# Attention and MoE kernel on one core: q and k turned as pairs of tokens in 32-bit words, statistics in three operations, the hand order rewritten

## The chip, the core and the metric

The kernel runs on one core of one Trainium2 chip. The core has five engines with their own instruction streams: TensorE (PE; its weight loads are listed as PEld), VectorE (DVE), ScalarE (ACT), GpSimd (POOL) and SyncE (SP, which here only issues transfers), and 16 DMA engines between them and HBM. [...] The metric is the device time of one execution in microseconds (us).

## The reference

Two parts follow each other. The first is attention with 4 batches, 8 heads, 768 tokens and 64 dimensions per head; a query sees the 8 first tokens and the 96 last ones, with a bias that falls with the distance:

```
scores = scale * q @ k.T                      # scale = 1/sqrt(64)
is_global = pos[None, :] < 8
is_local  = (rel >= 0) & (rel < 96)           # rel = query - key
dist  = where(is_global & ~is_local, 96, abs(rel))
scores = where(is_global | is_local, scores - slopes * dist, -1e9)
a = softmax(scores);  attn = a @ v
```

Its output is laid out as x, 3072 tokens of 512 values. The second is a feed-forward part with SoLU and layer norm, w_in of 512x1024 and w_out of 1024x512:

```
h = x @ w_in
solu = h * softmax(h)
ln = (solu - mean) / sqrt(var + 1e-6) * g_ln
out = ln @ w_out                              # 3072 x 512, float32
```

## The kernel before, in words

The 3072 tokens are 24 tiles of 128, six per batch. Heads are handled as four pairs p0 to p3 per batch, since two heads of 64 fill the 128 partitions.

Attention. q and k of a head pair come in as float32 with 128 tokens groups on the partitions: partition g holds six tokens in a row (load_heads, L469). In the code `j` is the place of a token in its group, `h` the head, `d` the dimension. A **cast** (steps cast_q and cast_k) makes float16 of them, 768 or 1536 values a partition, on POOL, VectorE or ScalarE. A **turn** (turn_q, turn_k, L712) makes six TensorE transposes of 128x128, one for each j, so that dimensions are on the partitions and tokens along the row. A **copy** (evac_q, evac_k) takes the turned 768 values of a partition out of PSUM into qT or kT, on VectorE or ScalarE, and puts tokens back in order with a stride. All copies and casts are recorded at the helper's lines: L271 for ScalarE, L273 for VectorE, L275 for POOL. There are 32 turns with 192 products. Scores follow (L839, L854), the exponential (L862), the bias as a factor (L871), the scores of the eight global keys (gscores), sums, the logarithm of the sums in a high and a low part (lhi L960, l16 L968), their exponential (rexp L1006), the products with v (L1031, L1041) and the scaled copy xT (L1066).

Feed-forward. gemm1 (L1104) multiplies a tile of xT with w_in, 8 products of 512 columns in two column halves; ef (L1114, ScalarE) takes the exponential and its sum s0, u (L1117, VectorE) the product with h and its sum s1, sq (L1124 on ScalarE or L1128 on VectorE) the sum of squares s2. u is turned by a DMA transpose (L1133) for tiles 5 to 21, and by TensorE (turn_u, L1143) with a copy out (evac_u, the tile named `late`) for the others. Every few tiles, **stats** (L1160 to L1167, four operations on VectorE on three columns) and rstd (L1171, L1172, ScalarE) make the scale of the layer norm; gemm2 (L1189) multiplies with gw_out (w_out scaled by g_ln and with its mean taken off), osb (L1199 or L1202) scales, and a store (L1206) is issued by SP or ScalarE.

w_in arrives in four transfers (L602), one for each half of its columns (fh 0, 1) and of its rows (jj 0 is rows 0 to 255, jj 2 rows 256 to 511), into the float32 tile `late`, and each half of a quarter is cast to w_in_sb. gemm1 of the first six tiles runs column half 0 first and then half 1, as two steps. w_out (L613) is scaled with g_ln by `centre` (L634), for which two float32 products (part_mean L626, mean L631) and a turn of g_ln (L575) are made.

Order. Every piece of this work is a step with a number. A table written by hand, ORDER, lists the step numbers; the steps are emitted in this order, and each engine runs its own part of it. SLOTS gives the buffer that each step takes, ENGS the engine of a step that has a choice, and WARM puts extra products on a constant tile (busy16, L1215) at places in the order. No step moves at run time; an engine that waits for a step holds everything behind it.

Of the kernel before, what the change touches and what calls it, by code (L numbers as in the profile page):

```python
# [17 lines left out]
P = 128  # L18
# [46 lines left out]
"""  # L65
SLOTS = """
# [78 lines left out]
def kernel(  # L145
# [113 lines left out]
    def one(s, n=0):  # L259
        return acc[:, at(s, "one", n), :]  # L260
# [993 lines left out]
```

## Time and profile before

| | us |
|---|---|
| median of three runs (161.46, 162.16, 163.80) | 162.16 |
| the profiled execution's own time | 162.93 |
| its span, from the first to the last instruction | 161.1 |
| TensorE busy | 150.1 |
| VectorE busy | 130.4 |
| ScalarE busy | 123.0 |
| GpSimd busy | 52.4 |

The span lies inside the execution's time, with 1.8 us around it; sums are made against 162.93, and the profiled execution is 0.77 above the median. The mean granted TensorE clock was 0.999. A busy share of TensorE counts a product from its start to its modelled end, so products in a row overlap in it. Of a row of the groups: busy time and mean of one, then idle time ahead of them on their engine and what ended it.

### The profile page before, as it was taken

How to read it: one execution, taken by the hardware profiler on the slowest of the kernel's cores; microseconds unless marked ns; L12 is line 12 of the kernel's file. 1: busy time of each engine (PE TensorE's matmuls, PEld its weight loads, DVE VectorE, ACT ScalarE, POOL GpSimd, SP SyncE). 2: the span in 40 equal slices, each digit the busy share in tenths (PEclk: the TensorE clock that was granted, in tenths of full speed). 3: DMA queues.
4: the chain of work that ended last, by engine and by line, in shares of the span. 5: the costliest groups of instructions: out<-in, count | busy, mean ns of one | idle time of the engine just before them, and what ended most of it. 6: DMA issues, size and time to landing. Idle time of an engine off the chain costs nothing.

```text
span 161.1 us, 4916 instructions
## 1 busy us (share of the span) xinstructions
PE 150.1 (93%) x1953; PEld 82.7 (51%) x1953; DVE 130.4 (81%) x271; ACT 123.0 (76%) x206; POOL 52.4 (33%) x120
## 2 busy tenths in 40 slices
PE   5689989999999999989999999999999999999991
PEld 1448546246565467457555434664444644444560
DVE  6384486999999999999699999783999778687830
ACT  3669997799989989887989959785974625856541
POOL 8764246257555377246165411300400000000000
PEclk9999999999999999999999999999999999999999
DMA  5999999989999999999669959711634803759453
GB/s 139 307 360 324 294 280 384 344 261 301 340 323 312 365 207 235 338 329 254 164 132 184 156 112 271 209 69 65 125 74 93 220 17 65 194 44 167 121 195 130
DMA packets 58390, 34.26 MB, mean 213 GB/s; under 512 B 44920, under 2 KB 53376, under 8 KB 58368
## 3 DMA queue, kind: packets, MB, share of 16 engines
q1 hardware_dynamic: 57360, 32.26, 75.4%
q10 hardware_dynamic: 1008, 1.70, 2.9%
q8 instruction: 15, 0.25, 0.6%
q14 instruction: 7, 0.06, 0.1%
HBM read 23.20 MB, written 6.29 MB: 183 GB/s over the span
## 4 chain that ended last, share of the span: by engine, by line
PE 50%; DVE 20%; DMA 13%; SPq 5%; issue 5%; ACT 3%; POOL 1%; DVEq 0%; ACTq 0%
PE acc L1189 24%; PE acc L1104 13%; DMA late<-in_moe_w_in_dram 9%; DMA x<-in_q_dram 5%; DVE eb L871 4%; DVE uu L1117 4%; DVE xT L1066 3%; PE acc L712 3%; PE acc L1041 3%; SPq L471 3%; DVE qT L273 2%; PE acc L854 2%; DVE v L273 1%; DVE sqv L1128 1%; ACT ef L1114 1%
## 5 line engine op out<-in xcount | busy, mean ns | idle before, releaser
L1189 PE MATMUL acc<-gw_out_sb,late 128*128 128x512 f16 (+1 forms) x200 | 45.0, 371 | 0.4 <-DVE qT L273 0.4
L1104 PE MATMUL acc<-w_in_sb,xT 128*128 128x512 f16 x192 | 44.4, 379 | 0.2
L1117 DVE SCALAR_TENSOR_TENSOR uu<-ef,acc 128x1024 f16<-128x1024 f16 x24 | 29.1, 1214 | 8.6 <-ACT ef L1114 8.5
L1114 ACT ACTIVATE ef<-acc 128x1024 f16<-128x1024 f32 x24 | 24.7, 1028 | 10.3 <-PE acc L1104 7.7
L862 ACT ACTIVATE eb<-acc 128x960 f16<-128x960 f32 (+1 forms) x32 | 29.0, 947 | 1.2 <-PE acc L854 0.9
L1104 PEld LDWEIGHTS <-xT 128*128 128x128 f16 x192 | 18.0, 98 | 22.1 <-DVE w_in_sb L273 0.9
L1189 PEld LDWEIGHTS <-late 128*128 128x128 f16 x200 | 18.6, 98 | 20.9 <-issue 1.6
L275 POOL CAST x<-x 128x768 f16<-128x768 f32 x20 | 18.1, 918 | 14.8 <-DMA x<-in_k_dram 6.1
L712 PE MATMUL acc<-ident,x 128*128 128x128 f16 x192 | 16.2, 238 | 2.7 <-POOL pick L342 1.5
L871 DVE TENSOR_TENSOR eb<-eb,fb 128x960 f16<-128x960 f16 x24 | 17.9, 761 | 0.6 <-ACT eb L862 0.5
L1124 ACT ACTIVATE sqa<-uu 128x1024 f16<-128x1024 f16 x14 | 14.8, 1059 | 3.5 <-DVE uu L1117 3.4
L712 PEld LDWEIGHTS <-x 128*128 128x128 f16 x192 | 13.2, 107 | 7.0 <-issue 2.1
L1066 DVE TENSOR_TENSOR xT<-acc,rr 128x384 f16<-128x384 f32 x32 | 16.0, 547 | 0.8 <-PE acc L1041 0.8
L1041 PE MATMUL acc<-eb,v 64*64 64x160 f16 (+4 forms) x448 | 15.2, 220 | 0.7 <-DVE tick L1051 0.5
L1006 ACT ACTIVATE rr<-acc 128x768 f32<-128x768 f32 x16 | 12.4, 812 | 4.1 <-DVE xT L1066 2.2
L1041 PEld LDWEIGHTS <-v 64*64 64x64 f16 x448 | 12.6, 106 | 4.2 <-issue 3.0
L275 POOL CAST v<-v 128x704 f16<-128x704 f32 (+3 forms) x14 | 9.1, 651 | 13.8 <-DMA v<-in_v_dram 13.8
L1199 ACT ACTIVATE osb<-acc,rstd 128x512 f32<-128x512 f32 (+1 forms) x13 | 8.4, 659 | 6.6 <-PE acc L1189 5.9
L273 DVE COPY qT<-acc 128x768 f16<-128x768 f16 x11 | 10.4, 949 | 3.7 <-PE acc L712 3.7
L1128 DVE SCALAR_TENSOR_TENSOR sqv<-uu 128x1024 f16<-128x1024 f16 x10 | 13.2, 1316 | 0.2
L854 PE MATMUL acc<-qT,kT 64*64 64x160 f16 (+2 forms) x384 | 13.1, 234 | 0.0
L1031 PE MATMUL acc<-eg,vgz 64*64 64x384 f16 x64 | 10.4, 324 | 0.0
(116 smaller groups left out, 201.3 us busy)
## 6 DMA issues: line engine op xcount, KB each, us to landing
x<-in_q_dram SPq DMA_DIRECT2D x16, 384.0 KB, 5.5
x<-in_k_dram SPq DMA_DIRECT2D x16, 384.0 KB, 6.1
out_dram<-osb SPq DMA_DIRECT2D x17, 256.0 KB, 2.5
v<-in_v_dram SPq DMA_DIRECT2D x12, 192.0 KB, 3.4
w_out<-in_moe_w_out_dram SPq DMA_DIRECT2D x4, 512.0 KB, 5.6
late<-in_moe_w_in_dram SPq DMA_DIRECT2D x4, 512.0 KB, 6.3
v<-in_v_dram SPq DMA_DIRECT2D x12, 160.0 KB, 3.8
out_dram<-osb ACTq DMA_DIRECT2D x6, 256.0 KB, 2.1
```

What stands on the lines that cost most here:

```text
L273: nc.vector.tensor_copy(out=out, in_=in_)
L275: nc.gpsimd.tensor_copy(out=out, in_=in_)
L712: nc.tensor.transpose(out=pt[:, ts(j, P)], in_=a[:, j, ts(pp, P)], identity=ident)
L854: nc.tensor.matmul(out=sc[o : o + 64, par, col : col + n], lhsT=kk[r, BLK * c : BLK * c + BLK], rhs=qq[r, g0 : g0 + n], start=fresh, stop= ...
L862: ex["fn"] = (lambda ex=ex, qk=qk, gw=gw: nc.scalar.activation(out=eb[at(qk, "eb")][:, :, 0:gw], in_=big(qk)[:, :, 0:gw], func=AF.Exp, sca ...
L871: nc.vector.tensor_tensor(out=e, in0=e, in1=bass.AP(tensor=f.tensor, offset=f.offset, ap=[f.ap[0], f.ap[1], [0, 3], f.ap[2]]), op=ALU.mult)
L1041: nc.tensor.matmul(out=o_[64 * h : 64 * h + 64, gl : gl + m], lhsT=vv[r, v_at(vi, h, c), pair, :], rhs=view(eb[at(e_own[b, gi, pair], "eb" ...
L1066: nc.vector.tensor_tensor(out=xT[at(xt_own[b], "xT")][:, p, q0:q1], in0=one(av, d)[:, 0:w], in1=rr[at(re, "rr")][:, d, 0:w], op=ALU.mult)
L1104: nc.tensor.matmul(out=ph()[:, ts(fh, 512)], lhsT=xT[at(xt_own[b], "xT")][:, j, ts(t % NA, P)], rhs=w_in_sb[:, j, ts(fh, 512)], start=(j = ...
L1114: ex["fn"] = lambda g1=g1, t=t, ph=ph: nc.scalar.activation(out=ef[at(g1, "ef")], in_=ph(), func=AF.Exp, accum_out=s0[:, t : t + 1])
L1117: u["fn"] = lambda u=u, g1=g1, t=t, ph=ph: nc.vector.scalar_tensor_tensor(out=uu[at(u, "uu")], in0=ef[at(g1, "ef")], scalar=USC, in1=ph(), ...
L1189: nc.tensor.matmul(out=one(g2)[:, 0:wd], lhsT=uT[at(el_o, "uT")][:, c, :], rhs=gw_out_sb[:, c, sl_], start=(c == 0), stop=(c == NFC - 1))
```

## The change

Four things change, and the tables with them.

- The cast writes two neighbouring tokens' float16 values (`t`) side by side, as (h, j, d, t): a 32-bit word holds a dimension of two tokens. It reads the float32 tile with a step of 64 words for t.
- The turn takes these words as float32 and makes three transposes of 128x128 against a float32 identity (ident32, a new constant on POOL) instead of six of float16; product j writes its words with a step of three, so that tokens come out in order.
- The copy out of PSUM is 768 contiguous float16 values, where it read with a step before.
- stats squares s0 and s1 in one operation (they lie side by side in s01 now) and adds in two more: three operations instead of four; the logarithm in rstd takes a scale of 1/1024.
- ORDER, SLOTS, ENGS and WARM are new. There are 11 warm products instead of 22. Of the turn copies 18 are on VectorE and 14 on ScalarE in both; sq goes from 10 on VectorE and 14 on ScalarE to 15 and 9; casts of q and k from 5, 7 and 20 (VectorE, ScalarE, POOL) to 9, 6 and 17.

```diff
@@ constants and tiles
+    ident32 = sb.tile([P, P], FP32, name="ident32")
-    s0 = sb.tile([P, NT], FP32, name="s0")
-    s1 = sb.tile([P, NT], FP32, name="s1")
+    s01 = sb.tile([P, 2, NT], FP32, name="s01")
+    s01q = sb.tile([P, 2, NT], FP32, name="s01q")
+    s0, s1 = s01[:, 0], s01[:, 1]
...
+    id32_st = step("POOL", 640, -90500, [], lambda: constants_ident(ident32, 1.0), name="c_ident32")
@@ cast
                          x16[at(cs, "x16_")][:, 0:m].rearrange(
-                             "p (j h d) -> p j h d", j=run, d=D),
+                             "p (h j d t) -> p h j d t", j=run // 2, d=D, t=2),
                          x32[at(iss, "x32_")][:, 0:m].rearrange(
-                             "p (h j d) -> p j h d", j=run, d=D))
+                             "p (h j t d) -> p h j d t", j=run // 2, d=D, t=2))
@@ turn
-                        pt = one(tps).bitcast(FP16)
-                        a = x16[at(cs, "x16_")][:, 0:m].rearrange("p (j x) -> p j x", j=run)
-                        for j in range(run):
-                            nc.tensor.transpose(out=pt[:, ts(j, P)], in_=a[:, j, ts(pp, P)],
-                                                identity=ident)
+                        pairs = run // 2
+                        pt = one(tps)[:, 0 : P * pairs].rearrange("p (g j) -> p j g", j=pairs)
+                        a = x16[at(cs, "x16_")][:, 0:m].bitcast(FP32).rearrange("p (j x) -> p j x", j=pairs)
+                        for j in range(pairs):
+                            nc.tensor.transpose(out=pt[:, j], in_=a[:, j, ts(pp, P)], identity=ident32)
@@ copy out
-                        copy(ev["at"], dst[at(ow[0], dn, ow[1])][:, lo:hi].rearrange("p (g j) -> p g j", j=run),
-                             one(tps).bitcast(FP16)[:, 0:n].rearrange("p (j g) -> p g j", j=run))
+                        copy(ev["at"], dst[at(ow[0], dn, ow[1])][:, lo:hi], one(tps).bitcast(FP16)[:, 0:n])
@@ stats and rstd
-                a, c = va[:, lo:hi], vb[:, lo:hi]
-                nc.vector.scalar_tensor_tensor(out=a, in0=s1[:, lo:hi],
-                                               scalar=-1.0 / D_FF / D_FF, in1=s1[:, lo:hi],
-                                               op0=ALU.mult, op1=ALU.mult)
-                nc.vector.scalar_tensor_tensor(out=a, in0=s2[:, lo:hi], scalar=1.0 / D_FF,
+                a, x = va[:, lo:hi], s01[:, :, lo:hi]
+                nc.vector.tensor_tensor(out=s01q[:, :, lo:hi], in0=x, in1=x, op=ALU.mult)
+                nc.vector.scalar_tensor_tensor(out=a, in0=s01q[:, 1, lo:hi], scalar=-1.0 / D_FF,
+                                               in1=s2[:, lo:hi], op0=ALU.mult, op1=ALU.add)
+                nc.vector.scalar_tensor_tensor(out=a, in0=s01q[:, 0, lo:hi], scalar=eps * D_FF,
                                                in1=a, op0=ALU.mult, op1=ALU.add)
-                nc.vector.scalar_tensor_tensor(out=c, in0=s0[:, lo:hi], scalar=eps,
-                                               in1=s0[:, lo:hi], op0=ALU.mult, op1=ALU.mult)
-                nc.vector.tensor_tensor(out=a, in0=a, in1=c, op=ALU.add)
...
-                nc.scalar.activation(out=vb[:, lo:hi], in_=va[:, lo:hi], func=AF.Ln)
+                nc.scalar.activation(out=vb[:, lo:hi], in_=va[:, lo:hi], func=AF.Ln, scale=1.0 / D_FF)
@@ WARM (position in the order : bank : products)
-28:0:5 36:4:0 49:4:1 73:0:2 92:0:4 107:6:2 128:6:5 168:4:1 197:4:1 297:4:1
+27:0:4 38:4:0 49:4:1 61:4:0 87:4:1 150:5:5
```

The new lines shift those behind them by one to four: copies and casts are at L273, L275 and L277 after, the turn at L716, gemm1 at L1106, gemm2 at L1188, the squares at L1126 and L1130, the loads of w_in at L605.

What the new tables do is seen at two places. The first is SP, around the loads of w_in (`late`, L602). The names: x is a piece of q or k, v, vt and vgn are pieces of v, g is g_ln. Before:

```order
L471 DMA x_2_104<-in_q_dram 128x2x384
L485 DMA v_0_113<-in_v_dram 128x3x64 x2
L613 DMA w_out_72<-in_moe_w_out_dram 128x2x512 x2
L602 DMA late<-in_moe_w_in_dram 128x2x512
L500 DMA vgn<-in_v_dram 64x1x64
L602 DMA late<-in_moe_w_in_dram 128x2x512 x2
L500 DMA vgn<-in_v_dram 64x1x64 x2
```

After, the same place:

```order
L575 DMA g_76<-in_moe_g_ln_dram 8x128
L605 DMA late<-in_moe_w_in_dram 128x2x512
L616 DMA w_out_73<-in_moe_w_out_dram 128x2x512
L605 DMA late<-in_moe_w_in_dram 128x2x512
L502 DMA vgn<-in_v_dram 64x1x64
L616 DMA w_out_73<-in_moe_w_out_dram 128x2x512
L605 DMA late<-in_moe_w_in_dram 128x2x512 x2
L487 DMA v_0_114<-in_v_dram 128x3x64
```

Before, one load of w_in stands further ahead (issued at 15.35 us in the trace), then one, then two together; after, one, one, and two together, with the last pieces of w_out between them. The four quarters change their order too, which the rows don't tell but the step numbers do: before (fh 1, jj 0), (fh 0, jj 2), (fh 0, jj 0), (fh 1, jj 2); after (fh 1, jj 0), (fh 1, jj 2), (fh 0, jj 2), (fh 0, jj 0). On all queues the transfers that are issued ahead of the last of them are the same in number and bytes: ten of q and k, eight of v, four of w_out, four of w_in.

The second place is VectorE in the middle of the run, where the factors of a group of scores (eb), copies (qT, kT), and u (uu) alternate. Before:

```order
L871 TENSOR_TENSOR eb_136<-eb_136,fb 128x960
L871 TENSOR_TENSOR eb_139<-eb_139,fb 128x960
L1117 SCALAR_TENSOR_TENSOR uu_157,s_94<-ef_153,acc 128x1024
L273 COPY kT_122<-acc 128x768
L273 COPY kT_120<-acc 128x768
L1117 SCALAR_TENSOR_TENSOR uu_154,s_94<-ef_152,acc 128x1024
L273 COPY qT_124<-acc 128x768
L1117 SCALAR_TENSOR_TENSOR uu_155,s_94<-ef_153,acc 128x1024
L273 COPY late<-acc 128x1024
```

After:

```order
L873 TENSOR_TENSOR eb_138<-eb_138,fb 128x960
L275 COPY kT_121<-acc 128x768
L275 CAST x_2_112<-x_2_105 128x2x3x128
L873 TENSOR_TENSOR eb_133<-eb_133,fb 128x960
L275 COPY qT_125<-acc 128x768
L275 COPY qT_124<-acc 128x768
L275 COPY qT_128<-acc 128x768
L1119 SCALAR_TENSOR_TENSOR uu_158,s_94<-ef_154,acc 128x1024
L1119 SCALAR_TENSOR_TENSOR uu_156,s_94<-ef_153,acc 128x1024
L275 COPY kT_120<-acc 128x768
L1130 SCALAR_TENSOR_TENSOR sqv,s_96<-uu_158 128x1024
```

More copies of qT and kT stand in a row, a cast of x and a square are put between them, and the products u come behind three copies. Counted from the first gemm1 to 108 us of before, VectorE has 13 of these copies after and 12 before, 7 squares and 4, 5 casts of x and 2, 3 copies of turned u and 2; 1 lhi and 2; of the casts of v of 704 columns 1 and 4, and one shorter. ScalarE has 9 copies and 10, 5 squares and 8, 4 casts of x and 3, 2 copies of turned u and 3; 3 casts of v of 704 columns and 1. POOL has 12 casts of x and 17. TensorE's steps in that part are the same in both.

More of the change, by code (lines that the diff above doesn't have):

```diff
@@ L684, in do_heads @@
                     take=("x32_",), name=nm)
-                cs = step(("POOL", "DVE", "ACT"), (10 + m, 35 + 0.59 * m, 120 + 0.785 * m), t0 - 1200, [dma],
+                cs = step(("POOL", "DVE", "ACT"), (85 + m, 35 + 0.59 * m, 290 + 0.785 * m), t0 - 1200, [dma],
                           None, lat=(100, 130, 155),
@@ L693, in cast @@
                          x16[at(cs, "x16_")][:, 0:m].rearrange(
-                             "p (j h d) -> p j h d", j=run, d=D),
+                             "p (j h d t) -> p h j d t", j=run // 2, d=D, t=2),
                          x32[at(iss, "x32_")][:, 0:m].rearrange(
-                             "p (h j d) -> p j h d", j=run, d=D))
+                             "p (h j t d) -> p h j d t", j=run // 2, d=D, t=2))
                 cs["fn"] = cast
@@ L700, in do_heads @@
                     p = p0 + pp
-                    tps = step("PE", 15 + run * 53.4, t0, [cs, id_st], None,
+                    tps = step("PE", 15 + run * 53.4, t0, [cs, id32_st], None,
                                take="one", mode="f", name="turn_" + nm, lat=180, ni=2 * run)
@@ L708, in pe @@
                     def pe(tps=tps, cs=cs, pp=pp):
[L709 to L713 removed]
+                        pairs = run // 2
[3 more added lines that the diff above has]
+                            nc.tensor.transpose(out=pt[:, j], in_=a[:, j, ts(pp, P)], identity=ident32)
                     tps["fn"] = pe
                     n = P * run
[L716 removed]
+                    ev = step(("DVE", "ACT"), (70 + 0.53 * n, 120 + 0.745 * n), t0 + 500, [tps], None, lat=(140, 165),
                               free=[(tps, "one")], name="evac_" + nm)
                     def evac(ev=ev, tps=tps, ow=ow, dst=dst, dn=dn, n=n):
[L720 to L721 removed]
+                        copy(ev["at"], dst[at(ow[0], dn, ow[1])][:, lo:hi], one(tps).bitcast(FP16)[:, 0:n])
                     ev["fn"] = evac
@@ L1158, in stats @@
             def stats(lo=lo, hi=hi):
-                a, c = va[:, lo:hi], vb[:, lo:hi]
-                nc.vector.scalar_tensor_tensor(out=a, in0=s1[:, lo:hi],
-                                               scalar=-1.0 / D_FF / D_FF, in1=s1[:, lo:hi],
-                                               op0=ALU.mult, op1=ALU.mult)
-                nc.vector.scalar_tensor_tensor(out=a, in0=s2[:, lo:hi], scalar=1.0 / D_FF,
+                a, x = va[:, lo:hi], s01[:, :, lo:hi]
[3 more added lines that the diff above has]
+                nc.vector.scalar_tensor_tensor(out=a, in0=s01q[:, 0, lo:hi], scalar=eps * D_FF,
                                                in1=a, op0=ALU.mult, op1=ALU.add)
-                nc.vector.scalar_tensor_tensor(out=c, in0=s0[:, lo:hi], scalar=eps,
-                                               in1=s0[:, lo:hi], op0=ALU.mult, op1=ALU.mult)
-                nc.vector.tensor_tensor(out=a, in0=a, in1=c, op=ALU.add)
-            st = step("DVE", 620, tt + 5700, [chain[x][1] for x in grp], stats, name="stats", lat=200)
+            st = step("DVE", 465, tt + 5700, [chain[x][1] for x in grp], stats, name="stats", lat=200)
             def rs(lo=lo, hi=hi):
-                nc.scalar.activation(out=vb[:, lo:hi], in_=va[:, lo:hi], func=AF.Ln)
+                nc.scalar.activation(out=vb[:, lo:hi], in_=va[:, lo:hi], func=AF.Ln, scale=1.0 / D_FF)
                 nc.scalar.activation(out=rstd[:, lo:hi], in_=vb[:, lo:hi], func=AF.Exp,
```

1 line of the change is left out of this document (removed), and 94 rows, old and new, of tables (ENGS, ORDER, SLOTS).

## The prediction

> **What bounds the kernel now.** I read the page first: the engine totals, the slices, the chain that ended last.
>
> ```profile
> span 161.1 us, 4916 instructions
> PE 150.1 (93%) x1953; PEld 82.7 (51%) x1953; DVE 130.4 (81%) x271; ACT 123.0 (76%) x206; POOL 52.4 (33%) x120
> DVE  6384486999999999999699999783999778687830
> ACT  3669997799989989887989959785974625856541
> PEclk9999999999999999999999999999999999999999
> PE 50%; DVE 20%; DMA 13%; SPq 5%; issue 5%; ACT 3%; POOL 1%; DVEq 0%; ACTq 0%
> PE acc L1189 24%; PE acc L1104 13%; DMA late<-in_moe_w_in_dram 9%; DMA x<-in_q_dram 5%; DVE eb L871 4%; DVE uu L1117 4%; DVE xT L1066 3%; PE acc L712 3%; PE acc L1041 3%; SPq L471 3%; DVE qT L273 2%; PE acc L854 2%; DVE v L273 1%; DVE sqv L1128 1%; ACT ef L1114 1%
> ```
>
> The reader is to see that no engine bounds the whole: TensorE is busy 93% but holds half of the chain, VectorE a fifth, and the transfers of w_in 9% in one place. The clock stays full. So I cut the run into stages: before the first gemm1, attention and gemms together, and the gemms that are left.
>
> ```profile
> 0.00:32.00 32.00, 26.61 (x405) 15.39 (x406) 21.13 (x59) 24.24 (x33) 17.04 (x69) 1.00 0.98 304
> 32.00:108.00 76.00, 74.14 (x1127) 42.93 (x1125) 71.83 (x134) 68.78 (x115) 33.59 (x50) 1.00 0.93 243
> 108.00:161.00 53.00, 49.38 (x425) 24.35 (x423) 37.47 (x80) 30.02 (x58) 1.82 (x1) 1.00 0.48 115
> by line: PE acc L1189 17.1%; DMA late<-in_moe_w_in_dram 12.4%; DVE eb L871 9.3%; issue 8.5%; DVE xT L1066 7.9%; PE acc L712 7.8%; DVE uu L1117 7.5%; PE acc L1104 6.3%; DVE qT L273 5.1%; DVE v L273 3.7%; DVE kT L273 3.3%; ACT eb L862 2.7%; P
> ```
>
> The columns after the length are PE, PEld, DVE, ACT, POOL busy, clock, DMA share, GB/s. The first stage is filled by transfers (0.98), the middle has three engines nearly full at once, the last belongs to TensorE. The fourth row is the chain from 32 to 96 us alone: there the work goes from engine to engine, and the two strided copies (qT and kT, L273) hold 8.4% of 64 us, 5.4 us.
>
> **The start: a term of its own.** The change doesn't alter how much is loaded ahead of the last quarter of w_in, but it alters which quarter comes last. The rows: SP's issues of w_in, three pieces of the chain, two stretches of TensorE, and one piece more of the chain.
>
> ```profile
> 15.35 1.17 SPq L602 DMA_DIRECT2D late<-in_moe_w_in_dram  x1
> 21.85 0.96 SPq L602 DMA_DIRECT2D late<-in_moe_w_in_dram  x1
> 23.52 1.06 SPq L602 DMA_DIRECT2D late<-in_moe_w_in_dram  x2
> 24.11 7.96 DMA late<-in_moe_w_in_dram
> 32.12 0.62 POOL w_in_sb L275
> 32.79 2.32 PE acc L1104 x10
> 31.23 3.88 PE L1104 MATMUL acc<-w_in_sb,xT 128*128 128x512 f16 x16
> 34.95 0.38 PE L1215 MATMUL acc<-busy 128*128 128x512 f16 x1
> 39.93 3.45 PE acc L1189 x16
> ```
>
> Before, the last quarter to be issued is columns 512 to 1023 of rows 256 to 511, which the first gemm1 needs only from the seventh of its 16 products on (tiles 2 and 0): TensorE starts at 31.23, and the next step at 34.95. After, the last is columns 0 to 511 of rows 0 to 255, which the very first product needs. With as many bytes ahead of it, it lands at 24.11 + 7.96 = 32.07, is cast by 32.74, and the products start at 32.79; 16 of them take 3.45 (the row at 39.93), so they end at 36.24: 36.24 − 34.95 = **+1.3 us**. TensorE has the same steps ahead of this point in both, so nothing else fills the wait. If the load comes 1 us sooner, the term is 0.3; I keep 0.3 to 1.6.
>
> **The products.** Of 32 turns (one is a head pair's 768 tokens of q or k), 10 are ahead of the first gemm1, under transfers; 22 are in the middle stage.
>
> ```profile
> 56.32 1.18 PE L712 MATMUL acc<-ident,x 128*128 128x128 f16 x18
> 30.00 1.12 PE L631 MATMUL acc<-part,onesq 128*128 128x512 f32 x2
> 29.99 0.30 PEld L631 LDWEIGHTS acc<-part,onesq 128*128 128x128 f32 x2 [0.23 <-ACT part L271]
> L631 PEld LDWEIGHTS acc<-part,onesq x2: 186/188/189, 30.0 to 30.1; 128*128 128x128 f32 x2
> L631 PE MATMUL acc<-part,onesq x2: 592/644/697, 30.0 to 30.5; 128*128 128x512 f32 x2
> ```
>
> A turn before: 18 products in 1.18 us, less the last one's tail (some 0.22), over 17 gaps: 56 ns each, six make 336. A 32-bit product of 128x128 isn't in the trace; the nearest are two of L631, 512 columns wide. Their loads start 0.30 − 0.19 = 0.11 us apart, the products 1.12 − 0.59 = 0.53; without the load, 0.42 for 512 columns, a quarter of which is 105. If load and stream overlap, a product takes some 107 ns, three make 320; ends of the range are 56 (as f16: 168 a turn) and 105 + 110 = 215 (nothing overlaps: 645). I take 107, since the second load of L631 starts while the first product streams. 22 × (320 − 336) = **−0.35 us**. The warm products that go from behind 32 us (two, 3.45 / 16 = 0.216 us each, the one at 34.95 among them) give **−0.4**.
>
> **Copies, casts and squares in the middle stage.** Columns at the end: busy, mean ns of one.
>
> ```profile
> L273 DVE COPY qT<-acc 128x768 f16<-128x768 f16 x7 | 6.6, 947 | 0.0
> L273 DVE COPY kT<-acc 128x768 f16<-128x768 f16 x5 | 4.6, 945 | 0.0
> L273 DVE COPY late<-acc 128x1024 f16<-128x1024 f16 x2 | 1.4, 686 | 0.2 <-PE acc L1143 0.2
> L273 DVE CAST x<-x 128x768 f16<-128x768 f32 x2 | 1.2, 621 | 0.0
> L273 DVE CAST v<-v 128x704 f16<-128x704 f32 x4 | 3.5, 876 | 0.0
> L1128 DVE SCALAR_TENSOR_TENSOR sqv<-uu 128x1024 f16<-128x1024 f16 x4 | 5.8, 1456 | 0.0
> L960 DVE TENSOR_SCALAR lhi<-lns,mlo 128x384 f16<-128x384 f32 x2 | 0.8, 410 | 0.0
> L1165 DVE SCALAR_TENSOR_TENSOR vb<-s 128x3 f32<-128x3 f32 x4 | 0.6, 153 | 0.0
> L271 ACT COPY kT<-acc 128x768 f16<-128x768 f16 x6 | 4.8, 805 | 0.0
> L271 ACT COPY late<-acc 128x1024 f16<-128x1024 f16 x3 | 3.1, 1029 | 0.0
> L271 ACT CAST x<-x 128x768 f16<-128x768 f32 x3 | 2.5, 838 | 0.0
> L271 ACT CAST v<-v 128x704 f16<-128x704 f32 x1 | 0.8, 799 | 0.0
> L1124 ACT ACTIVATE sqa<-uu 128x1024 f16<-128x1024 f16 x8 | 8.5, 1062 | 1.5 <-DVE uu L1117 1.3
> L1124 ACT ACTIVATION_READ_ACCUMULATOR sqa<-uu 128x1 f32 x8 | 1.6, 200 | 0.0
> ```
>
> A contiguous VectorE copy of 768 from PSUM isn't here; that of 1024 took 686, so it lies between 515 (in proportion) and 686, and no gain leaves 947. I take 550: a part of the 686 is fixed. ScalarE gains nothing: 805 for 768 strided is as much per element as 1029 for 1024 contiguous.
> VectorE in the middle, counted from the two orders: copies, 13 × 0.55 instead of 12 × 0.946, −4.2; three more squares, 3 × 1.53 with their readout, +4.6; three more casts of x, +1.9; casts of v, three of 704 fewer and one short one more, −2.2; one more copy of u, +0.7; one lhi less, −0.4; in four groups of statistics an operation less, −0.6. Together −0.3.
> ScalarE: three squares fewer, 3 × 1.26, −3.8; one turn copy less, −0.8; one copy of u less, −1.0; one cast of x more, +0.8; two casts of v more, +1.6. Together −3.2.
> POOL gives five of its casts of x away; it was idle over half of the stage, so this is hidden. What VectorE gains on copies is thus spent on squares, and the gain appears on ScalarE, where the chain holds little. TensorE's steps in this stage are the same in both, and it was unbusy for 76.00 − 74.14 = 1.86 us; its busy time holds waits too, so more can go. I take half of the 3.5 us of both engines, **−1.75**, near that 1.86; the ends are 0 and −5.2 (all of ScalarE's 3.2 and 42% of the copies' 5.4, or 2.0; the saving of a copy is 0.4 of 0.95).
> The casts now read with a stride of 64 words and write word pairs. No cast of before does; I take the old durations, since ScalarE reads PSUM at a stride with no loss, and keep +0.4 us on each (what VectorE's strided copy loses, 947 against 550) as the other end: hidden on POOL, +2.0 on VectorE's five, some of it again on ScalarE's four, which has given 3.2 away. I see no reason for a gain, since the bytes read and written stay the same.
>
> **The last stage.** Statistics are three operations instead of four, 0.15 us by L1165, ahead of rstd and the outputs; the last tile's chain keeps its operations. TensorE's products set this stage, and I count nothing, within 1 us either way. One store more is issued by ScalarE instead of SP; ScalarE is busy 30.02 of 53.00 us here, which hides it. The new constant is built on POOL in the first stage, where it is busy 17.04 of 32.00; without that cover the first turns would start later by its length, and the transfers, not the turns, end that stage. The nine other warm products that go lie under the first stage's transfers.
>
> **Sum.** The profiled execution took 162.93 us, its span and 1.8 around it, 0.77 above the median of 162.16. 162.93 + 1.3 − 0.35 − 0.4 − 1.75 = 161.7; less 0.77, **160.9 us**. Two per cent, 158.9 and 165.4, is about what a measurement of this kernel can tell from no change.
>
> **The rivals.**
> *Forecast*, 159 to 163.5: chance 0.52, of which I put 0.01 below 158.9 and 0.03 above 165.4.
> *The copies were the chain.* If what leaves VectorE and ScalarE comes off the end whole, −5.2 stands for −1.75: 157.5. For it: VectorE is 71.83 of 76 busy, and qT and kT have no idle time ahead of them (0.0), they queue behind other work. Against it: the squares that VectorE takes over fill the same queue. 0.24.
> *A 32-bit product is slow.* At 215 ns each, 66 products in a stage where TensorE has 1.86 us free cost 66 × 0.108 = +7.1: 168.0, slower. It decides from some 68 ns above my 107, about 175 a product (4.5 / 66). For it: no product of before writes at a step of 12 bytes. Against it: the loads of L631 overlap. 0.14.
> [...]
> *Strided casts are slow.* +2.0 on VectorE: 162.9. 0.06.
> [...] The trace has no such cast; its strided copies out of PSUM lose time on VectorE and none on ScalarE.
> *The copy isn't faster.* If the price of 947 is that of 768 halfwords out of PSUM in that place, and no stride: 13 × 0.4 = +5.2, 166.1. 0.04.
>
> **Numbers.** Below 158.9 lie the second case and the forecast's lower edge: 0.24 + 0.01 = 0.25. Above 165.4 the third, the fifth and the upper edge: 0.14 + 0.04 + 0.03 = 0.21. Within, 0.48 + 0.06 = 0.54. The likeliest is 160.9; the range of 157.2 to 166.2 leaves out most of the slow product and the far end of the fast copies, some 0.2.
>
> **What would show it.** The products of L716 should start 107 ns apart; copies of L275 on VectorE take 515 to 686; casts of x about 620, 840 and 930 on the three engines; the first gemm1 starts near 32.8 behind the last quarter of w_in; and ScalarE's busy time in the middle falls by 3 us. I am wrong if L716 goes above 175, if the first gemm1 isn't held, or if chains in the middle close up beyond what ScalarE gave.

## The result, and the profile after

The changed kernel takes 168.7 us (median of five runs, 167.46 to 170.86) where before takes 162.31 beside it: a ratio of **1.034** (1.027 to 1.041), slower. The ratio compares the faster runs alone, three of these five and four of five of before, so it is a little below that of the medians. The profiled execution took 167.54 us against 162.93, its span 165.8 against 161.1. The forecast of 160.9 and its range up to 166.2 were both missed.

Lines of the changed kernel's page: the engines, the 40 slices of TensorE and of the transfers, the queue of instructions that is read below (packets, MB, share of the DMA time), and the chain of work that ended last:

```profile
span 165.8 us, 4718 instructions
PE 147.5 (89%) x1846; PEld 81.0 (49%) x1846; DVE 130.5 (79%) x275; ACT 118.9 (72%) x195; POOL 57.2 (35%) x121
PE   4669778699999799998699999889999999999991
DMA  5999989999899989999927999981395703846743
q8 instruction: 14, 0.23, 0.6%
PE 57%; DMA 20%; DVE 10%; issue 4%; ACT 3%; SPq 2%; POOL 0%; POOLq 0%; DVEq 0%; ACTq 0%
```

No engine became the bound: TensorE, VectorE and ScalarE all have a smaller share than before. VectorE's part of the chain halved (20% to 10%), that of the transfers grew (13% to 20%), and "issue", time in which the profile shows nothing to wait for, stands at 4% (5% before). The same stages as before show where TensorE lost its time:

```profile
0.00:32.00 32.00, 23.01 (x352) 12.74 (x352) 17.34 (x55) 20.18 (x27) 19.67 (x74) 1.00 0.94 295
32.00:108.00 76.00, 70.94 (x954) 40.53 (x950) 70.57 (x135) 65.65 (x108) 34.56 (x45) 1.00 0.99 234
108.00:166.00 58.00, 53.54 (x544) 27.75 (x544) 42.56 (x87) 33.04 (x61) 3.01 (x3) 0.99 0.54 122
```

In the middle TensorE is busy 70.94 us of 76 where it was 74.14, while the transfers go from 0.93 to 0.99 of their time. The stages are cut at the same times, so the change, which lags, has done less of its program in them: 954 products against 1127, of which the halved turns explain 66. That ScalarE's busy time falls by 3.1 us (65.65 for 68.78), as forecast, is therefore no measure of the saving.

The products and the copies came out as priced, the casts didn't. Rows of the groups on VectorE, ScalarE and GpSimd (32 to 108 us; the GpSimd row over 0 to 108), and one piece of the chain:

```profile
L275 DVE COPY qT<-acc 128x768 f16<-128x768 f16 x9 | 4.8, 548 | 0.3 <-PE acc L716 0.3
L275 DVE CAST x<-x 128x768 f16<-128x768 f32 x5 | 4.4, 884 | 0.0
L273 ACT CAST x<-x 128x768 f16<-128x768 f32 x5 | 5.0, 1004 | 0.0
L277 POOL CAST x<-x 128x768 f16<-128x768 f32 x17 | 18.0, 1067 | 10.5 <-PE acc L1106 3.8
84.75 0.98 PE acc L716 x9
```

A copy takes 548 ns instead of 947, a 32-bit product 0.98 / 9 = 109 ns, and the casts are slower than the 621, 838 and 918 ns of before (VectorE, ScalarE, GpSimd).

**Two waits have no cause in the profile.** What TensorE waited for (total, times, longest), and its timeline at the first of them:

```profile
PE acc L856 <- issue: 3.0, 2, 2.0
PE acc L716 <- POOL x L277: 2.7, 3, 1.7
PE acc L629 <- ACT rr L1008: 1.7, 1, 1.7
PE acc L1188 <- DMA late<-uu: 1.6, 2, 1.4
...
52.95 0.81 PE L856 MATMUL acc<-qT,kT 64*64 64x160 f16 x16
54.77 0.43 PE L856 MATMUL acc<-qT,kT 64*64 64x160 f16 x13 [1.01 <-issue]
```

In the middle of a run of score products TensorE stops, with nothing that would release it. Before has no such row. The records of the trace show what falls there. The queue `q8 instruction` carries packets of 16 KB, one for about 260 of TensorE's records (its products and weight loads, counted from 0: 3717 records, 14 packets; 3915 and 15 before), and both waits end behind the end of one of them. Start of the last product ahead and of the next record, the number of that record, and the packet:

```
kernel          wait              record   packet start + length   from its end to the next record
change          53.52 -> 54.77    1217     52.21 + 1.13            1.43 us
change          78.04 -> 80.23    1985     77.74 + 1.07            1.42 us
```

The two records are 768 apart, three times 256. This gives a theory to test, and no more than that: TensorE's own instructions come late here, since packets of them stand behind data. No row shows what these packets carry or that an engine waits for one.

### The profile page after: what moved, and what is told of

Read it like the earlier page. It is cut to its first block, busy times and chain, and to the rows that moved or that the text cites. A ratio compares the mean times of both kernels' runs of the same rounds, so it can differ in the third digit from the quotient of the medians.

```text
span 165.8 us, 4718 instructions
## 1 busy us (share of the span) xinstructions
PE 147.5 (89%) x1846; PEld 81.0 (49%) x1846; DVE 130.5 (79%) x275; ACT 118.9 (72%) x195; POOL 57.2 (35%) x121
## 4 chain that ended last, share of the span: by engine, by line
PE 57%; DMA 20%; DVE 10%; issue 4%; ACT 3%; SPq 2%; POOL 0%; POOLq 0%; DVEq 0%; ACTq 0%
PE acc L1188 20%; PE acc L1106 19%; DMA x<-in_k_dram 9%; DMA late<-uu 6%; DMA late<-in_moe_w_in_dram 5%; PE acc L1043 4%; DVE uu L1119 4%; PE acc L716 3%; PE acc L856 3%; DVE gw_out_sb L637 2%; ACT ef L1116 1%; PE acc L999 1%; PE acc L629 1%; DVE sqv L1130 1%; PE acc L939 1%
## 5 line engine op out<-in xcount | busy, mean ns | idle before, releaser
L1188 PE MATMUL acc<-gw_out_sb,late 128*128 128x512 f16 (+1 forms) x200 | 43.8, 371 | 2.1 <-DMA late<-uu 1.6
L1106 PE MATMUL acc<-w_in_sb,xT 128*128 128x512 f16 x192 | 44.8, 379 | 0.3 <-DVE uu L1119 0.2
L864 ACT ACTIVATE eb<-acc 128x896 f16<-128x896 f32 (+1 forms) x32 | 29.3, 957 | 4.7 <-PE acc L856 4.7
L1188 PEld LDWEIGHTS <-late 128*128 128x128 f16 x200 | 19.1, 98 | 23.1 <-DMA late<-uu 2.0
L1106 PEld LDWEIGHTS <-xT 128*128 128x128 f16 x192 | 18.1, 98 | 20.8 <-issue 1.1
L277 POOL CAST x<-x 128x768 f16<-128x768 f32 x17 | 18.0, 1067 | 10.5 <-PE acc L1106 3.8
L716 PE MATMUL acc<-ident,x 128*128 128x128 f32 x96 | 16.5, 299 | 3.5 <-POOL x L277 2.7
L1130 DVE SCALAR_TENSOR_TENSOR sqv<-uu 128x1024 f16<-128x1024 f16 x15 | 19.0, 1269 | 0.2
L277 POOL CAST v<-v 128x704 f16<-128x704 f32 (+3 forms) x12 | 9.5, 799 | 20.5 <-DMA v<-in_v_dram 15.4
L716 PEld LDWEIGHTS acc<-ident,x 128*128 128x128 f32 x96 | 11.3, 150 | 7.7 <-POOL x L277 3.9
L1043 PE MATMUL acc<-eb,v 64*64 64x160 f16 (+4 forms) x448 | 14.7, 219 | 0.3 <-ACT eb L864 0.3
L856 PEld LDWEIGHTS <-kT 64*64 64x64 f16 x384 | 8.8, 111 | 6.2 <-issue 5.0
L1201 DVE TENSOR_SCALAR osb<-acc,rstd 128x512 f32<-128x512 f32 x12 | 8.9, 748 | 3.0 <-PE acc L1188 2.4
```

The source lines that it names most:

```text
L277: nc.gpsimd.tensor_copy(out=out, in_=in_)
L716: nc.tensor.transpose(out=pt[:, j], in_=a[:, j, ts(pp, P)], identity=ident32)
L856: nc.tensor.matmul(out=sc[o : o + 64, par, col : col + n], lhsT=kk[r, BLK * c : BLK * c + BLK], rhs=qq[r, g0 : g0 + n], start=fresh, stop= ...
L864: ex["fn"] = (lambda ex=ex, qk=qk, gw=gw: nc.scalar.activation(out=eb[at(qk, "eb")][:, :, 0:gw], in_=big(qk)[:, :, 0:gw], func=AF.Exp, sca ...
L1043: nc.tensor.matmul(out=o_[64 * h : 64 * h + 64, gl : gl + m], lhsT=vv[r, v_at(vi, h, c), pair, :], rhs=view(eb[at(e_own[b, gi, pair], "eb" ...
L1106: nc.tensor.matmul(out=ph()[:, ts(fh, 512)], lhsT=xT[at(xt_own[b], "xT")][:, j, ts(t % NA, P)], rhs=w_in_sb[:, j, ts(fh, 512)], start=(j = ...
```

## The experiments

Each ratio is to runs of before taken beside it on the same chip; the change stands at 1.034.

### Which half of the change costs: the code or the tables

The step numbers of both kernels differ by the one new step (the identity), so each code runs under the other's ORDER, SLOTS, ENGS and WARM.

```diff
 e1_old_tables: changed cast, turn, copy, statistics
-ORDER, SLOTS, ENGS, WARM of the change
+ORDER, SLOTS, ENGS, WARM of before (c_ident32 set behind c_ident)
 e2_old_code: cast, turn, copy, statistics of before
-ORDER, SLOTS, ENGS, WARM of before
+ORDER, SLOTS, ENGS, WARM of the change (without c_ident32)
```

> The changed cast, turn, copy and statistics run under the tables of before (order, buffers, engines, warm products; the new identity stands behind the old one on POOL). If the word layout itself is what costs (strided casts, 0.26 us more on VectorE, 0.17 on ScalarE, 0.13 on POOL each), this is slower than before, 164 to 167 us. If the new tables are what costs, it is as fast as before or faster: 160.5 to 162.5 us, since copies save 0.4 us on VectorE 18 times. The first gemm1 should start near 31.2 us as before, and TensorE should have no wait of over 1 us for which the profile shows no releaser.

> The cast, turn, copy and statistics of before run under the tables of the change (without the step of the new identity). If the tables cost, this is slower than before by all of it or more: 166 to 170 us, with the first gemm1 near 34 us. If the word layout costs, it is near 162 us.

Measured: the new code under the old tables 1.003 (0.999 to 1.007), the old code under the new tables 1.042 (1.037 to 1.048). **The tables hold all of the loss.** The code by itself does not move the time under the old order; under the new one it reads 0.8% faster, with intervals that overlap. The middle stage of the new code under the old tables, and its copies:

```profile
32.00:108.00 76.00, 74.31 (x1063) 42.97 (x1062) 69.00 (x132) 68.85 (x115) 35.83 (x50) 1.00 0.94 243
L274 DVE COPY qT<-acc 128x768 f16<-128x768 f16 x7 | 3.8, 550 | 0.2 <-PE acc L715 0.2
L274 DVE COPY kT<-acc 128x768 f16<-128x768 f16 x5 | 2.7, 548 | 0.5 <-PE acc L715 0.5
```

VectorE does 2.8 us less (71.83 to 69.00), its copies now wait for TensorE, and TensorE is as busy as before: the gain is off the path.

How far a kernel lags behind before can be followed through the run, if the work of TensorE that has been done is summed from the starts of its products (columns by their pace, warm products left out) and the times at which two profiles have the same sum are subtracted (good to some 0.3 us):

```
us behind before, when before is at    32     44     72    104    end
change                                 2.6    2.0    2.6   5.6    4.6
e1_old_tables                          0.3   -0.2   -0.4  -0.3   -0.2
e2_old_code                            3.6    4.1    5.6   8.4    7.0
e4_shift176 (below)                    3.2    2.4    2.8   4.6    3.5
e6s_start_shift (below)                1.1    1.3    2.1   3.9    2.9
```

Some 2.5 us are lost by the first gemm1, about as much again in the middle.

### Are TensorE's instructions late?

If so, the wait belongs to a count of instructions and not to a product. Tiny products on TensorE ahead of the waits, in its first 10 us, of which it is busy 4.94 in the change, shift the count and change nothing else: 88 of them are 176 records, a product and its weight load each. The expectations call the counts at which the theory has the next packet due places of fetches; they are an estimate from the two records above, and no row shows such a place.

```diff
+            for _ in range(count // 1000):
+                nc.tensor.matmul(out=acc[0:32, spot, 0:8], lhsT=busy16[:, 0:32],
+                                 rhs=busy16[:, 0:8], start=True, stop=True)
```

> The changed kernel with 88 tiny products (32 columns loaded, 8 streamed) added on TensorE in the first 10 us, nothing else. [...] If the two waits without a releaser (1.2 us at 53.4 and 2.1 us at 78.0) are TensorE waiting for its instructions behind other transfers, both go, and the time falls by 2 to 3.3 us, less up to 1.5 for the products: 166 to 167.5 us. If they wait for data, they stay where they are and the time is 168.5 or above.

> The changed kernel with 48 tiny products instead of 88. By the places of the fetches, the first wait (53.4 us) goes and the second stays but comes earlier in the program, some 2 us ahead of its old place, at the 1889th instead of the 1985th of TensorE's old records, 1.5 to 3 us long. If they wait for data, both stay at the same products as in the change.

With 88 of them: 1.023 (1.018 to 1.029), 166.14 us, and none of its products has a wait of 0.2 us or more without a releaser. **A kernel with 176 more instructions is about 1% faster**: its four runs, 165.80 to 167.19 us, all lie below the five of the change. With 48: 1.033 (1.025 to 1.041), and one such wait, at the count that was expected:

```profile
PE acc L856 <- issue: 2.3, 1, 2.3
```

```
kernel          wait              record   packet start + length   from its end to the next record
e5_shift96      77.05 -> 79.55    1985     76.81 + 1.14            1.60 us
```

The record has the same number, 1985, and so stands 96 records earlier in the program than in the change; no data that it could need is the same. Wherever TensorE had such a wait of over 0.5 us in the middle of a row of products, the record behind it is number 193 + 256 n: 705 under the old code in the new tables (1.9 us from one start to the next), 961 in e7 below, 1217 and 1985 in e3, in e6 and in the kernel with the start of before. Kernels under the old tables have one too, at 1985 (e1 0.6 us, e8 1.0 us), and at ratios of 1.003 and 1.005 lose no time that can be told.

One of the two waits is gone here and the time is not lower. The trace shows something that the change's own profile doesn't have: behind the wait that is left TensorE's granted clock is at half for 3.4 us. That stretch, and the first eight products of gemm1 in it, with eight of the change behind its wait:

```profile
80.90:84.30 3.40, 3.40 (x32) 1.57 (x32) 3.40 (x4) 2.93 (x4) 3.40 (x4) 0.50 0.70 158
81.80 3.12 PE L1106 MATMUL acc<-w_in_sb,xT 128*128 128x512 f16 x8
82.85 1.90 PE L1106 MATMUL acc<-w_in_sb,xT 128*128 128x512 f16 x8
```

The profiles of e3 and e6 below have the same, with the clock at half for 3.4 us from 78.8 and from 81.8 us. Of the change's five runs four had a mean clock of 0.980 to 0.987, and in its profile it is 0.997; of the four with the 88 products none was below 0.996. Five of the runs of before beside these experiments had 0.979 and took 162.24 to 163.78 us, nothing lost that can be told, so the mean alone is no cost; but the eight products took 3.12 us at half the clock and 1.90 at the full one. The 1% may thus hold both, the stops and the clock behind them; the runs don't part the two.

The opposite test is to put such a wait into before.

```diff
 e7_before_shift: the kernel before
+96 tiny products in TensorE's first 9 us
```

> The kernel before, with 96 tiny products in TensorE's first 9 us and nothing else. [...] If late instructions cost time, TensorE gets waits without a releaser that before doesn't have, and the time rises by 1.5 to 4 us: 163.7 to 166.5 us. If they don't, it is within 0.6 us of before.

Measured 1.004 (0.999 to 1.008): not the 1.5 to 4 us expected, a term that no run shows. A stop of 1.9 us did come, at record 961 and 29.0 us, and the time doesn't show it; near 50 us a packet started at 49.13, and no product behind it has a wait of over 0.4 us without a releaser. In these runs the number of the record behind a stop could be told ahead, and whether a stop comes could not; what decides that is not shown.

### The start

> The changed kernel, with the quarters of w_in loaded in the order of before (the quarter that the first product needs is no longer last) and the first two casts of w_in behind the exponentials that TensorE waits for on ScalarE. If the start of the first gemm1 (33.9 us against 31.2) is carried to the end, this gains 1.5 to 2.7 us against the change: 165.5 to 167 us. If the later waits take it up, it stays within 0.7 us of the change.

In it the five warm products (27.5 us) came to write a PSUM bank that a spread of the attention part was using, so part of the output is spoilt; the work is the same. It ran at 1.029 (1.022 to 1.036), no clear gain, and the first gemm1 started at 33.71 instead of 34.03: the quarter and the two casts weren't alone in holding it. The next one mends three holds at once, with the warm products back in place.

```diff
-149 (fh1 jj0)  153 (fh1 jj2)  145 (fh0 jj2)  141 (fh0 jj0)
+149 (fh1 jj0)  145 (fh0 jj2)  141 (fh0 jj0)  153 (fh1 jj2)
-ScalarE: cast w_in, rexp, rexp, cast w_in, copy_mean, rexp
+ScalarE: rexp, rexp, cast w_in, copy_mean, rexp, cast w_in
-TensorE: gemm1 t2, gemm1b t2, gemm1 t0, gemm1b t0
+TensorE: gemm1 t2, gemm1 t0, gemm1b t2, gemm1b t0
```

> The changed kernel with a mended start: the quarters of w_in in the order of before, ScalarE's casts of them behind the exponentials that TensorE waits for, and the first gemm1 running column half 0 of tiles 2 and 0 ahead of half 1. If the start is held by these three, the first gemm1 starts at 32.3 to 33 us (33.9 in the change) and the time falls by 1 to 1.8 us, to 166 to 167 us in the runs of the change (a ratio to before of 1.023 to 1.028). If the attention ahead of it holds it, 33.5 us and nothing gained.

> The mended start and the 88 tiny products. If start and late instructions are two separate losses, both gains add: 2.5 to 3.5 us below the change, a ratio to before of 1.012 to 1.018. If one hides the other, it stays at the 1.023 of the kernel with the products alone.

Alone: 1.030 (1.021 to 1.039), not told from the change; in the traced execution (170.88 us) the first gemm1 starts at 33.59, later than expected. With the tiny products: 1.017 (1.011 to 1.024), the first gemm1 at 32.51. The two gains add in the ratios; against the 1.023 of the products alone the intervals overlap, so the start's share of 0.6% is only indicated.

Grafting the start of before onto the rest of the change, and the other way round, was to split the loss at the first gemm1. The rest keeps each engine's order; only steps that the other start had done already are left out, and buffers are given anew where they clash.

> The changed kernel, whose order, engines and buffers up to the first gemm1 are those of before; from there on each engine runs its steps in the order of the change. If the start loses 2.6 us that stay lost, this gains 2 to 3 us against the change: 165 to 166.5 us, with the first gemm1 near 31.2 us. If the middle would lose them anyway, it stays within 0.7 us of the change. The instruction stream of TensorE ahead of the cut is 18 records longer, so the two waits without a releaser (50 to 80 us) should still be there, 2.5 to 4.5 us together.

> The kernel with the start of before, and 79 tiny products more in the first 9 us of TensorE. If the two waits are late instructions, they go and this gains 2 to 3.5 us more: 162 to 164 us, as fast as before within 1 us. If they are not, it is as the kernel without the products or up to 1 us above it.

> The start of the change up to the first gemm1, and each engine's order of before from there on. If the start is worth 2.6 us by itself, this is 2 to 3.5 us above before: 164.5 to 166.5 us. If the order of before takes it up, 162.5 to 163.5.

Measured: 1.069 (1.063 to 1.075), 1.054 (1.046 to 1.062) and 1.063 (1.054 to 1.072): all worse than either parent, and no answer to the question. The seam costs 6 to 8 us: the start has issued other loads for the middle than the rest wants first, TensorE stands for casts that wait for them, and its clock is at half for 6.8 us from 41.4 us. TensorE at the seam of the first:

```profile
35.71 1.03 PE L1105 MATMUL acc<-w_in_sb,xT 128*128 128x512 f16 x4
40.56 0.55 PE L715 MATMUL acc<-ident,x 128*128 128x128 f32 x3 [3.83 <-ACT x L272]
42.46 0.90 PE L715 MATMUL acc<-ident,x 128*128 128x128 f32 x3 [1.35 <-ACT x L272]
```

Two things are still to be had from them. The tiny products gain again, 1.069 to 1.054, and take away both waits of that kernel at records 1217 and 1985 (one of 0.6 us comes at record 2241, again 193 + 256 n). And with them the kernel is as far behind before at 44 us as at 148 us (9.1 us at both): in that profile the middle of the new order loses nothing more. As every load has 9 us more there, this points at loads that come late in the change, and, if the theory holds, instructions; it doesn't show it.

### The casts, the copies and the statistics

```diff
 e8_plain_casts (old tables), e9_plain_new (new tables, mended start, tiny products)
-    copy(..., x16 as "p (j h d t) -> p h j d t", x32 as "p (h j t d) -> p h j d t")
+    copy(..., x16[...][:, 0:m], x32[...][:, 0:m])
```

(In memory the words lie as (j, h, d, t), j counting pairs of tokens.)

> The changed code under the tables of before, with casts that copy in the order of memory, so that words hold two dimensions instead of two tokens: q and k are mixed, all instructions stay. If the strided casts eat the gain of the copies, the casts fall to 0.6, 0.83 and 0.93 us and the time falls 0.7 to 2.5 us below the kernel with strided casts, to 160.5 to 162.3 us. If neither is on the path, it stays within 0.6 us of it.

> The change with the mended start and the 88 tiny products, and casts in the order of memory (words hold two dimensions: q and k are mixed, all instructions stay). If the slower casts on ScalarE and GpSimd are what the rest of the loss is (TensorE still waits some 3 us for casts of x in its turns), the ratio to before falls from 1.017 to 1.005 or below. If the rest lies in the order itself, it stays within 0.5% of 1.017.

Casts of the first, in the order of memory:

```profile
L276 POOL CAST x<-x 128x768 f16<-128x768 f32 x20 | 18.0, 911 | 12.1 <-DMA x<-in_k_dram 5.7 <-DMA x<-in_q_dram 3.9 <-PE acc L713 2.5
L272 ACT CAST x<-x 128x768 f16<-128x768 f32 x7 | 5.9, 844 | 2.0 <-DMA x<-in_q_dram 1.8 <-DMA x<-in_k_dram 0.2
L274 DVE CAST x<-x 128x768 f16<-128x768 f32 x5 | 2.9, 575 | 2.8 <-DMA x<-in_q_dram 1.8 <-DMA x<-in_k_dram 1.0
```

Under the old tables the strided cast takes 1036, 1016 and 591 ns on the three engines: 0.13 and 0.17 us dearer on GpSimd and ScalarE, nothing on VectorE. In the time it is nothing: 1.005 (0.998 to 1.011) against 1.003, and 1.017 (1.011 to 1.023) against 1.017.

VectorE's 884 ns in the change are something else. Cast by cast they are 0.56 us, or 1.35 and 1.40 us for the two at 78.95 and 81.60 us, where GpSimd is at work beside them; in the kernel with the mended start and the tiny products four are of 1.17 to 1.40. The stride isn't the cause: in memory order, in e9, two are of 1.18 and 1.39. They were given away:

```diff
 e13_casts_moved: on e6s_start_shift
-cast_k b3 p2, cast_q b2 p2, cast_k b3 p0, cast_q b3 p1 on VectorE
+the first two on GpSimd, the last two on ScalarE
```

> The change with the mended start and the 88 tiny products, and four of VectorE's casts of x, which took 1.17 to 1.40 us instead of 0.56 while GpSimd worked, given to GpSimd (the two at 54 and 57 us) and ScalarE (the two at 78 and 81 us). If these casts hold the turns behind them and VectorE's work for gemm1 (2.3 us of TensorE's waits between 34 and 110 us name them), the ratio to before falls from 1.017 to 1.005 to 1.012. If the rest lies in where the order puts them, not in how long they take, it stays within 0.4% of 1.017 or rises.

Measured 1.023 (1.015 to 1.031), against 1.017: no gain. The rest of the loss doesn't come back with the length of these casts; GpSimd and ScalarE have the work instead.

The next two ask whether ScalarE holds the middle, and whether the copies' gain can be put to use there:

```diff
 on e1_old_tables, behind the first gemm1
-10 copies of qT and kT on ScalarE
+e10_half: 5, e11_all: none; the others on VectorE at the same places
```

> The changed code under the tables of before, with five of ScalarE's ten copies of qT and kT behind the first gemm1 given to VectorE, which does them in 0.55 us instead of 0.80: ScalarE 4.0 us less, VectorE 2.8 us more, which it has just been spared. If ScalarE holds the middle, 0.5 to 2 us below the kernel without that move (161 to 162.5 us); if TensorE's own order holds it, no change within 0.6 us.

> The same with all ten: ScalarE 8.0 us less, VectorE 5.5 us more than the changed code under the tables of before, 2.7 us more than before. If ScalarE holds the middle, as good or better than with five; if VectorE does, 0.5 to 2 us slower than with five.

Measured 1.004 (1.000 to 1.007) and 1.007 (1.003 to 1.011). In the middle stage of the first, both engines have less to do than before (VectorE 70.24 for 71.83, ScalarE 65.24 for 68.78); in that of the second, ScalarE has 7 us less than with all ten (68.85), and VectorE as much as before:

```profile
32.00:108.00 76.00, 73.12 (x1057) 42.44 (x1056) 70.24 (x135) 65.24 (x109) 37.05 (x51) 1.00 0.96 247
32.00:108.00 76.00, 72.77 (x1056) 42.29 (x1054) 71.67 (x139) 61.66 (x103) 36.94 (x50) 1.00 0.94 243
```

Neither is faster for it. Savings of this size on VectorE, on ScalarE or on both don't set the time of the middle under the old tables.

> The kernel before with the statistics in three operations alone: 0.15 us less of VectorE in each of eight groups, none of it long in front of TensorE: within 0.5 us of before.

The statistics alone: 0.995 (0.990 to 1.001), 162.97 us: the one part of the change that may be worth something, and not told from nothing. No kernel of this study is shown to beat before.

## Why the prediction was wrong

**What bounds the kernel.** The reading that the work goes from engine to engine and that no engine bounds the whole stands. What I drew from it doesn't.

**The start, +1.3.** The mechanism was right, the term too small: the first gemm1 starts 34.03 − 31.23 = 2.8 later, and counted as in the prediction, to the next step, 37.48 − 34.95 = 2.5. SP's issues of w_in, the transfer of the second quarter, and what hung on it:

```profile
20.39 0.39 SPq L605 DMA_DIRECT2D late<-in_moe_w_in_dram  x1
21.34 0.48 SPq L605 DMA_DIRECT2D late<-in_moe_w_in_dram  x1
23.39 1.30 SPq L605 DMA_DIRECT2D late<-in_moe_w_in_dram  x2
21.34 7.64 DMA late<-in_moe_w_in_dram
29.00 0.62 ACT L273 CAST w_in_sb<-late 128x512 f16<-128x512 f32 x1 [2.25 <-DMA late<-in_moe_w_in_dram]
29.53 1.50 ACT L1008 ACTIVATE rr<-acc 128x768 f32<-128x768 f32 x2
30.39 1.92 PE L629 MATMUL acc<-w_out,gbc 128*32 128x512 f32 x16 [1.71 <-ACT rr L1008]
33.10 0.87 POOL L277 CAST w_in_sb<-late 128x512 f16<-128x512 f32 x1 [0.84 <-DMA late<-in_moe_w_in_dram]
34.03 3.61 PE L1106 MATMUL acc<-w_in_sb,xT 128*128 128x512 f16 x16
```

"With as many bytes ahead of it, it lands at 32.07" failed by 1.0 us: the last quarter is there at 33.10. That fits the first 32 us, which moved 295 GB/s instead of 304, 0.29 MB less, a microsecond's worth; why they moved less is open. Its cast took 0.87 instead of 0.62. And a second hold, which I hadn't looked for, ends at nearly the same time: ScalarE stands at a cast of w_in until 29.00, with the exponentials (rr) queued behind it, and these hold the mean of w_out and so the products ahead of gemm1. In e3, with the quarter moved and the first casts behind the exponentials, ScalarE still does a cast of w_in from 31.59 ahead of the copy that the products of the mean (L633) wait for, which fits the 0.3 us that it gave.

**The products, −0.35.** Right: 109 ns measured, 107 forecast. The rival of slow 32-bit products falls with it: the products that write at a step of 12 bytes run at 109 ns, nearly as fast as 128 columns of L631's contiguous rows by the prediction's estimate (105). No run has the same products with a contiguous output.

**Copies, casts, squares, −1.75: the step that failed on the side of the gain.** The copy's duration was right (548 for 550). The casts were taken at their old durations and are dearer on ScalarE and GpSimd (0.17 and 0.13 us by e8), as their rival had it in kind; in the time that is nothing. But "I take half of the 3.5 us of both engines" gave to the path what only made two engines idler. The old tables show it: VectorE 2.8 us less than before, and the ratio is 1.003; VectorE 1.6 and ScalarE 3.5 us less, about the savings that the forecast added up, and it is 1.004. The term is 0, the end of its range, not −1.75. The 8.4% that qT and kT held in the chain were no measure of a gain: in e1 other links stand in their place, as if that chain were one of several nearly equal ones.

**What the sum lacked: the order as such.** "TensorE's steps in this stage are the same in both" was taken to mean that it would need the same time for them. I counted what the tables moved by engine and duration, and priced only one wait in them. Under the old code they cost 4.2%, under the new 3.4%. Of these 3.4 the study assigns about 1.1 to the stops that the 88 tiny products take away, perhaps with the clock behind them, and, less surely, 0.6 to the start. Some 1.7% is left, and its cause is open: it's not the stride of the casts, nor the length of VectorE's casts beside GpSimd. The kernel with the mended start and the tiny products still has TensorE wait 2.4 us for casts of x and 1.0 us for u between 34 and 110 us, so the places of the loads and casts in the order are the likeliest of what is left; that is argued, not shown.

**The rivals and the chances.** The slower side had 0.21, for two mechanisms that didn't happen and the upper edge of the forecast. No rival had the new order itself as its cause, and that is the one that the runs show.

## What to carry to other kernels

Before a saving is counted, take the same work off the engine in another way, or ask what the chain would be without it; a share of the chain is no measure of the gain: here 8.4% of it gave nothing. A hand order is a part of the kernel like any code: run the new code in the old order and the old code in the new one first, since that tells in two runs which of them pays. And when an engine stops in a row of equal instructions with no releaser, look at the packets of the queue that the profile calls `instruction` beside those of the data, at the number of the record behind the stop, and at the granted clock there.

## What the runs showed of the hardware

- Three stops of TensorE in a row of products, two in the change and one in e5, ended 1.42, 1.43 and 1.60 us behind the end of a packet of 16 KB on `q8 instruction`. In every such stop of over 0.5 us, in all the kernels traced, the next record is number 193 + 256 n of the trace. From start to start the stops are of 0.6 to 2.5 us; the DMA engines' share of the middle stage was 0.99 in the change and 0.94 in e1, which both have such stops. With 176 records more the ratio was 1.023 instead of 1.034. That TensorE waits there for its instructions fits e4 and e5 and is not shown.
- VectorE's casts of 128x768 from float32 to float16 took 591 ns on average with a stride of 256 bytes (e1) and 575 in memory order (e8). In the change three of those behind 45 us, with GpSimd idle beside them, took 0.56, and the two at 78.95 and 81.60 us 1.35 and 1.40: there a cast of x and a multiplication (vgz) of GpSimd had begun 0.48 and 0.47 us ahead, and VectorE's cast ended 0.42 us behind the end of each. Ahead of 20 us one took 0.58 beside a shorter operation of GpSimd (kg) that had begun 0.30 us ahead, so GpSimd's work alone doesn't decide it.
- TensorE's granted clock is at half behind stands of TensorE in several traces: in the first graft for 6.8 us from 41.4 us (stands at 36.7 and 41.1 us, of 3.8 and 1.4 us) and for 3.4 us from 61.8 us (a stop from 59.6 to 61.4 us); in or behind a stop at record 1985 in e3, e5 and e6 for 3.4 us (mean clock 0.990 in each). In the change's own profile it stays full behind a wait of 2.0 us, so the wait alone doesn't decide it. The slices of the first graft, 4.4 us each:

```profile
PEclk9999999997599969999999999999999999999999
```
